# A sliding-window attention and token-MLP block on one core: single matmuls between the scores, six value blocks placed from PSUM, a new instruction order

## The chip, the cores and the metric

The kernel runs on one core of a Trainium2 chip. The time is device time in microseconds, the median of three executions. A profile is taken of one further execution; its trace gives for every engine what ran when. The engines are TensorE (PE, with its weight loads shown apart as PEld), VectorE (DVE), ScalarE (ACT), GpSimd (POOL) and SyncE (SP, which issues the transfers). Each takes its instructions in the order in which they were written for it, and waits where an input isn't there yet.

## The reference

The input x has 2048 tokens of 512 features. A vector c gives six modulation vectors. The block is a windowed attention with 32 heads of 16 features, followed by an MLP that mixes tokens (2048 tokens to 1792 hidden units and back, for each feature):

```python
mod = (_silu(c) @ w_mod).reshape(c.shape[0], 6, 1, -1)      # sa, ca, ga, sb, cb, gb
h = _layernorm(x) * (1 + ca) + sa
qkv = (h @ wqkv) ...                                        # q, k, v of 32 heads of 16
scores = einsum('bhqd,bhkd->bhqk', q, k) * Dh ** (-0.5)
mask = (i - j >= 0) & (i - j < 256)
x = x + ga * (softmax(where(mask, scores, -1e9)) @ v) @ wo
h = _layernorm(x) * (1 + cb) + sb
u = gelu(einsum('bsd,sf->bdf', _layernorm(h), w1) + b1)
x = x + gb * (einsum('bdf,fs->bds', u, w2) + b2).transpose
```

Inputs, weights and result are bf16.

## The kernel before

The tokens are worked on in four groups of 512 (`G` from 0 to 3), the heads in four sets of eight (`g8`). For each token group `proj` normalizes x (`xn`), transposes it by DMA into `h1T`, scales and shifts `h1T`, and makes Q, K and V with TensorE. A 512-wide product over the 512 features is four matmuls that add up in one PSUM bank (`pq`, `pk`, `pv`).

K and V have to be laid out with zeros between heads, so that a matmul over 32 rows meets one head only. K is cast out of PSUM into `kb` (by ScalarE or VectorE), and two instructions with the mask `mask_par` write it into `KT`. V is cast into `vb`, and two instructions with `mask_half` (the function `place`) write it into `VT`. GpSimd, which has most of these, reads the copies `kb` and `vb`.

The attention is cut into 75 chunks, counted from 0 in this text. For a chunk TensorE writes four banks of scores: three banks `pss` (one buffer) and one bank `psb` (two buffers). ScalarE exponentiates them with two instructions, `et<-pss` and `et<-psb`; the next chunk's scores can go into `pss` once the first of the two is done. VectorE multiplies the result with the window mask (`et<-et,maskt`). A unit (256 queries for one set of heads) takes the pieces of two or three chunks. Once their masks are done, TensorE multiplies with `VT` and with a matrix of ones (`po`), which gives the values and the softmax sums; ScalarE makes the reciprocal as exp(-ln) (`lz`, two instructions), and VectorE multiplies (`OT`).

`post` multiplies with the output weights (`pa`), adds the residual, normalizes (statistics `st`, then `mv`, `sq`, `rs`, `nm`; then `h`), multiplies and shifts by the modulation (`h<-h,bc_cb`, `h<-h,bc_sb`, in the text a pair of products), normalizes again and writes `hb`. From `hb` and the first MLP weights (`w1s`, `w1r`) come the hidden units `pu`: part of the sums over tokens is made early and kept in `part`, the rest follows after the attention. The tail then has Gelu (`g`), the product `guT`, and the second MLP matmul `py`, 238 matmuls with the residual added at the end.

What sets the order around all this: every step is an `Op`, made with the engines that may run it and a planned cost for each, in the order of the program. `run_schedule` emits the ops in the order of the table `ORDER`, on the engine that the table `CHOSEN` names (else the first one allowed). `Ordered` keeps each engine's instructions in that order, so all have the helper's line, L259, in the profile. Three PSUM banks (`bank`, "od") are handed round among all products that aren't scores; a new product waits for the cast that empties its bank.

TensorE's work is of three kinds: scores use it as four row tiles, values and V as four column tiles, dense products as a whole. A run of dense matmuls next to column-tiled ones is itself cut into four column tiles (`mm` with `Op.quad`), if it isn't longer than `NEAR_RUN` ops between two of them. Before, an op of a dense product holds two matmuls:

```python
for dc in (2 * n, 2 * n + 1):
    mm(
        box["q", g8][:], wqkv[:, dc, g8 * P : (g8 + 1) * P], h1T[:, dc, :],
        (dc == 0), (dc == ND - 1),
    )
...
a, z = dense("q", [0.431] * 2, e_q, h_ops, pos, alloc="od", ready=10.0)
```

## Time and profile before

| | before |
|---|---|
| median of three | 254.7 us (254.2 to 254.94) |
| profiled execution | 254.84 us |
| its span, first to last instruction | 253.1 us |
| granted TensorE clock | 0.999 |
| busy: PE, DVE, ACT, POOL | 234.0, 204.3, 179.2, 132.4 us |
| DMA | 26.86 MB, mean 106 GB/s |

The page first gives the busy time of each engine, then the span in 40 slices:

```profile
PE   7987788999988889999899899999999999999995
DVE  5597999987999989969998989899969774444443
ACT  4598999999999999999999999998138510000000
POOL 8279959999999996497159049982000000000000
```

Each digit is the busy share of 6.3 us in tenths. The first two slices are the start; ScalarE's row of nines up to about 170 us is the attention; behind it TensorE's nines stand alone.

A row of the view by line or shape reads: line, engine, operation, output and inputs by the program's names, shapes, count, busy time, mean of one in ns, then the engine's idle time just before such instructions and what ended most of it. A timeline row has the start, the length, the engine and the instruction; in brackets the idle time before it and what ended it ("issue" is a wait that the profile can't name). Rows with "x n" are n instructions in a row. A busy matmul isn't TensorE at its peak, since matmuls are pipelined.

### The profile page before, as it was taken

How to read it: one execution, taken by the hardware profiler on the slowest of the kernel's cores; microseconds unless marked ns; L12 is line 12 of the kernel's file. 1: busy time of each engine (PE TensorE's matmuls, PEld its weight loads, DVE VectorE, ACT ScalarE, POOL GpSimd, SP SyncE). 2: the span in 40 equal slices, each digit the busy share in tenths (PEclk: the TensorE clock that was granted, in tenths of full speed). 3: DMA queues.
4: the chain of work that ended last, by engine and by line, in shares of the span. 5: the costliest groups of instructions: out<-in, count | busy, mean ns of one | idle time of the engine just before them, and what ended most of it. 6: DMA issues, size and time to landing. Idle time of an engine off the chain costs nothing.

```text
span 253.1 us, 9991 instructions
## 1 busy us (share of the span) xinstructions
PE 234.0 (92%) x4385; PEld 131.6 (52%) x4385; DVE 204.3 (81%) x398; ACT 179.2 (71%) x253; POOL 132.4 (52%) x231
## 2 busy tenths in 40 slices
PE   7987788999988889999899899999999999999995
PEld 2765556655665454555555455556444444444443
DVE  5597999987999989969998989899969774444443
ACT  4598999999999999999999999998138510000000
POOL 8279959999999996497159049982000000000000
PEclk9999999999999999999999999999999999999999
DMA  6999254540173000031114821122999301111111
GB/s 204 324 351 289 52 81 26 85 109 3 23 143 93 3 5 3 3 88 44 57 33 111 225 72 52 56 84 83 295 395 386 130 23 41 41 53 50 47 41 41
DMA packets 40227, 26.86 MB, mean 106 GB/s; under 512 B 12024, under 2 KB 36088, under 8 KB 40184
## 3 DMA queue, kind: packets, MB, share of 16 engines
q1 hardware_dynamic: 40176, 26.23, 36.8%
q8 instruction: 34, 0.56, 1.0%
q14 instruction: 9, 0.07, 0.1%
q10 hardware_dynamic: 8, 0.00, 0.0%
HBM read 22.03 MB, written 2.10 MB: 95 GB/s over the span
## 4 chain that ended last, share of the span: by engine, by line
PE 39%; ACT 23%; POOL 22%; issue 7%; DVE 3%; DMA 2%; SPq 2%; POOLq 0%
ACT et L259 20%; PE py L259 19%; PE pu L259 11%; POOL h L259 7%; POOL KT L259 3%; PE pss L259 3%; POOL VT L259 3%; ACT lz L259 3%; DMA x<-in_A_x_dram 2%; POOL h1T L259 2%; POOL sq L259 2%; PE po L259 2%; POOL rs L259 2%; SPq L259 2%; PE pa L259 1%
## 5 line engine op out<-in xcount | busy, mean ns | idle before, releaser
L259 ACT ACTIVATE et<-pss 128x1536 bf16<-128x1536 f32 x75 | 111.0, 1480 | 3.9 <-PE psb L259 3.1
L259 PE MATMUL py<-guT,w2r 128*128 128x512 bf16 (+2 forms) x238 | 48.5, 366 | 0.0
L259 DVE TENSOR_TENSOR et<-et,maskt 128x1024 bf16<-128x1024 bf16 (+2 forms) x79 | 47.8, 623 | 0.4 <-ACT et L259 0.2
L259 ACT ACTIVATE et<-psb 128x512 bf16<-128x512 f32 x75 | 47.2, 630 | 0.0
L259 PE MATMUL pu<-hb,w1s 128*32 128x512 bf16 (+1 forms) x308 | 39.0, 380 | 0.7 <-POOL hb L259 0.5
L259 PE MATMUL pss<-QT,KT 32*128 32x64 bf16 (+3 forms) x720 | 30.3, 230 | 8.9 <-ACT et L259 6.0
L259 PEld LDWEIGHTS <-w2r 128*128 128x128 bf16 x238 | 22.8, 98 | 25.9
L259 PE MATMUL po<-et,VT 128*32 128x64 bf16 (+3 forms) x960 | 32.2, 233 | 1.6 <-DVE kb L259 1.1
L259 PEld LDWEIGHTS <-KT 32*128 32x128 bf16 x960 | 17.2, 92 | 30.5 <-issue 27.8
L259 PE MATMUL po<-et,ones_bd 128*32 128x256 bf16 (+3 forms) x624 | 31.4, 268 | 0.0
L259 DVE TENSOR_TENSOR otile<-py,xr 128x512 bf16<-128x512 f32 (+2 forms) x17 | 11.2, 660 | 24.4 <-PE py L259 24.3
L259 PE MATMUL psb<-QT,KT 32*128 32x64 bf16 (+3 forms) x240 | 29.4, 231 | 0.0
L259 POOL TENSOR_SCALAR VT<-vb,mask_half 128x512 bf16<-128x512 bf16 x30 | 23.3, 786 | 7.9 <-DVE vb L259 6.7
L259 PEld LDWEIGHTS <-VT 128*32 128x32 bf16 x960 | 21.8, 97 | 10.3 <-issue 3.6
L259 POOL TENSOR_SCALAR KT<-kb,mask_par 128x512 bf16<-128x512 bf16 (+1 forms) x32 | 22.4, 713 | 5.2 <-DVE kb L259 5.1
L259 PEld LDWEIGHTS <-w1s 128*32 128x32 bf16 (+1 forms) x308 | 14.2, 96 | 16.4 <-issue 2.5
L259 DVE BATCH_NORM_STATS2 st<-x 128x6 f32<-128x512 bf16 x32 | 21.4, 682 | 1.7 <-DMA x<-in_A_x_dram 1.6
L259 PE MATMUL pk<-h1T,wqkv 128*32 128x512 bf16 (+4 forms) x240 | 20.5, 342 | 2.4 <-issue 1.1
L259 PEld LDWEIGHTS <-wqkv 128*32 128x32 bf16 (+1 forms) x434 | 15.3, 96 | 11.8 <-issue 5.6
L259 PE MATMUL pv<-wqkv,h1T 128*32 128x256 bf16 x512 | 18.1, 274 | 0.2
L259 PE MATMUL pu<-hb,w1r 128*32 128x512 bf16 (+1 forms) x120 | 18.2, 379 | 0.0
L259 PE MATMUL pa<-wod,OT 128*32 128x512 bf16 (+1 forms) x148 | 16.6, 381 | 0.4 <-DVE part L259 0.2
(105 smaller groups left out, 351.5 us busy)
## 6 DMA issues: line engine op xcount, KB each, us to landing
w2r<-in_B_w_dram SPq DMA_DIRECT2D x14, 512.0 KB, 10.8
w1s<-in_B_w_dram SPq DMA_DIRECT2D x19, 256.0 KB, 3.6
w1r<-in_B_w_dram SPq DMA_DIRECT2D x9, 256.0 KB, 4.6
x<-in_A_x_dram SPq DMA_DIRECT2D x16, 128.0 KB, 4.9
wmod<-in_w_mod_dram SPq DMA_DIRECT2D x4, 512.0 KB, 7.2
out_dram<-otile SPq DMA_DIRECT2D x15, 128.0 KB, 1.7
wmod<-in_w_mod_dram SPq DMA_DIRECT2D x4, 256.0 KB, 3.6
wqkv<-in_A_wqkv_dram SPq DMA_DIRECT2D x4, 256.0 KB, 5.4
```

The lines of the kernel that those rows point to most:

```text
L259: ins = call(*args, **kwargs)
```

## The change

An op of a dense product now holds one matmul in place of two (`q`, `k`, `pa`, `pu`, the early `part` sums); for V, two of the four feature blocks of a half. The value products and the sums of a unit are two ops, `e_av` and `e_sum`, where they were one. `NEAR_RUN` goes from 7 to 14. Six of the V blocks (`DIRECT_V`: two for each of the token groups 1 to 3) are placed into `VT` straight from PSUM by two instructions, without `vb`, and give up their bank after the second. The planner is told that ScalarE may place K and V (`masked`) and normalize. `DIRECT_K`, the same for K, is empty. `ORDER` and `CHOSEN` are new. The arithmetic is the same.

```diff
-NEAR_RUN = 7
+NEAR_RUN = 14
+DIRECT_V = [(1, 2), (1, 3), (2, 2), (2, 3), (3, 2), (3, 3)]
+DIRECT_K = []
 ORDER = [
-    46, 44, 47, 45, 48, 49, 51, 50, 52, 65, 53, 119, 66, 54, 120, 75, 67, 70, 55, 68, 71, 121, 76, 69, 56, 72, 123,
+    46, 44, 47, 45, 48, 49, 51, 50, 52, 65, 53, 127, 66, 54, 128, 75, 67, 76, 55, 68, 70, 129, 71, 69, 56, 131, 72,
...
+        elif e == "ACT":
+            ac.activation(out=dst, in_=src, func=ACT.Identity, scale=rs[:, i : i + 1], bias=nm[:, i : i + 1])
...
-    def values(dst, h1T, tb, n):
+    def values(dst, h1T, tb, n, dcs):
-        for dc in range(ND):
+        for dc in dcs:
...
+    def masked(e, out, in_, mask):
+        if e == "ACT":
+            ac.activation(out=out, in_=in_, func=ACT.Copy, scale=mask)
+        else:
+            ENGINE[e].tensor_scalar(out=out, in0=in_, scalar1=mask, scalar2=0.0, op0=ALU.mult, op1=ALU.add)
...
-                for dc in (2 * n, 2 * n + 1):
-                    mm(
-                        box["q", g8][:], wqkv[:, dc, g8 * P : (g8 + 1) * P], h1T[:, dc, :],
-                        (dc == 0), (dc == ND - 1),
-                    )
+                mm(box["q", g8][:], wqkv[:, n, g8 * P : (g8 + 1) * P], h1T[:, n, :], (n == 0), (n == ND - 1))
-            a, z = dense("q", [0.431] * 2, e_q, h_ops, pos, alloc="od", ready=10.0)
+            a, z = dense("q", [0.2155] * 4, e_q, h_ops, pos, alloc="od", ready=10.0)
...
+            if (G, tb) in DIRECT_V:
+                placed = [
+                    op("vd", {"ACT": 0.5, "DVE": 0.61}, 0.5,
+                       lambda e, half=half: place(e, VT[r3], box["v", tb], tb, half), deps=[z] + war, pos=pos)
+                    for half in range(2)
+                ]
+                a.frees = placed
...
-        engine, shifted = ({"POOL": 0.77, "DVE": 0.35}, True) if G < POOL_POST else ({"DVE": 0.34}, False)
+        engine, shifted = ({"POOL": 0.77, "DVE": 0.35, "ACT": 0.5}, True) if G < POOL_POST else ({"DVE": 0.34}, False)
...
+        for cost, emit, needs in ((0.005 + 0.0001 * len(mine), e_av, vs), (0.007 + 0.0001 * len(runs), e_sum, [])):
+            av = op("AV", "PE", columns + cost, emit, deps=ready + needs + av_chain[-1:],
+                    pos=i + AV_POS, cls="AV", alloc=None if unit["avs"] else "od")
...
-            for sc in range(lo, NT, 2):
+            for sc in range(lo, NT):
```

How the new tables move instructions is seen on the engines that wait for each other. In all, VectorE has 12 placings `VT<-pv` where it had none, 6 V casts fewer, 3 Q casts fewer (they go to ScalarE) and 4 pairs of products fewer; GpSimd has 12 V placings and 6 K placings fewer and those 4 pairs more; TensorE has 66 matmuls more, since more of the dense products are cut into column tiles.

ScalarE, in the first chunks. `et<-pss` and `et<-psb` are the exponentials of a chunk; before:

```order
L259 ACTIVATE et<-pss 128x1536
L259 ACTIVATE et<-psb 128x512
L259 ACTIVATE rs<-mv,eps_t 128x2
L259 ACTIVATE rs<-rs 128x2
L259 ACTIVATE kb<-pk 128x256
L259 ACTIVATE et<-pss 128x1536
L259 ACTIVATE et<-psb 128x512
L259 ACTIVATE et<-pss 128x1536
L259 ACTIVATE et<-psb 128x512
L259 ACTIVATE vb<-pv 128x512
L259 ACTIVATE et<-pss 128x1536
```

and with the change:

```order
L279 ACTIVATE et<-psb 128x512
L279 ACTIVATE QT_1_148<-pk 128x256
L279 ACTIVATE rs<-mv,eps_t 128x2
L279 ACTIVATE rs<-rs 128x2
L279 ACTIVATE QT_2_149<-pk 128x256
L279 ACTIVATE et<-pss 128x1536
L279 ACTIVATE kb<-pk 128x256
L279 ACTIVATE et<-psb 128x512
L279 ACTIVATE et<-pss 128x1536
L279 ACTIVATE QT_3_150<-pk 128x256
L279 ACTIVATE vb<-pv 128x512
L279 ACTIVATE et<-psb 128x512
```

Three Q casts are new among the first three chunks. On TensorE, in the same place, 8 of the 16 K/Q matmuls between the scores of chunks 3 and 4 move behind those of chunk 4.

VectorE, around the masks of chunks 23 to 26 (the V of token group 2 is `VT_169`), before:

```order
L259 CAST vb<-pv 128x512
L259 TENSOR_TENSOR et<-et,maskt 128x4x256
L259 CAST kb<-pk 128x512
L259 TENSOR_TENSOR et<-et,maskt 128x4x128
L259 CAST vb<-pv 128x512
L259 TENSOR_SCALAR h_2314<-x_68,rs,nm 128x512
L259 TENSOR_SCALAR h_2337<-x_67,rs,nm 128x512
L259 TENSOR_TENSOR et<-et,maskt 128x4x256
L259 CAST vb<-pv 128x512
L259 TENSOR_TENSOR h_2314<-h_2314,bc_cb_118 128x512
L259 TENSOR_TENSOR h_2314<-h_2314,bc_sb 128x512
```

and with the change:

```order
L279 CAST kb<-pk 128x512
L279 TENSOR_TENSOR et<-et,maskt 128x4x256
L279 TENSOR_SCALAR VT_169<-pv,mask_half 128x32x16
L279 TENSOR_TENSOR OT_0_140<-po,lz 128x256
L279 TENSOR_SCALAR VT_169<-pv,mask_half 128x32x16
L279 TENSOR_SCALAR h_2401<-x_68,rs,nm 128x512
L279 CAST QT_1_148<-pq 128x512
L279 TENSOR_TENSOR et<-et,maskt 128x4x128
L279 TENSOR_TENSOR et<-et,maskt 128x4x256
L279 TENSOR_SCALAR VT_169<-pv,mask_half 128x32x16 x2
```

Two V casts became four placings from PSUM, and the pair of products went to GpSimd.

GpSimd, in the same stretch, before:

```order
L259 TENSOR_SCALAR KT_3_162<-kb,mask_par 128x16x32 x2
L259 TENSOR_SCALAR h_2351<-x_66,rs,nm 128x512
L259 TENSOR_SCALAR VT_169<-vb,mask_half 128x32x16 x2
L259 TENSOR_SCALAR h_2439<-x_65,rs,nm 128x512
L259 TENSOR_TENSOR h_2337<-h_2337,bc_cb_118 128x512
L259 TENSOR_TENSOR h_2337<-h_2337,bc_sb 128x512
L259 TENSOR_SCALAR KT_1_164<-kb,mask_par 128x16x32 x2
L259 TENSOR_TENSOR h_2351<-h_2351,bc_cb_118 128x512
L259 TENSOR_TENSOR h_2351<-h_2351,bc_sb 128x512
L259 TENSOR_SCALAR VT_169<-vb,mask_half 128x32x16 x2
L259 TENSOR_SCALAR KT_0_163<-kb,mask_par 128x16x32 x2
L259 TENSOR_SCALAR VT_169<-vb,mask_half 128x32x16
```

and with the change:

```order
L279 TENSOR_SCALAR KT_3_162<-kb,mask_par 128x16x32 x2
L279 TENSOR_TENSOR h_2314<-h_2314,bc_cb_118 128x512
L279 TENSOR_TENSOR h_2314<-h_2314,bc_sb 128x512
L279 TENSOR_SCALAR xn<-x_80,rs,nm 128x512
L279 TENSOR_SCALAR h_2581<-x_66,rs,nm 128x512
L279 TENSOR_TENSOR h_2581<-h_2581,bc_cb_118 128x512
L279 TENSOR_TENSOR h_2581<-h_2581,bc_sb 128x512
L279 TENSOR_TENSOR h_2736<-h_2736,bc_cb_118 128x512
L279 TENSOR_TENSOR h_2736<-h_2736,bc_sb 128x512
L279 TENSOR_SCALAR KT_0_163<-kb,mask_par 128x16x32 x2
L279 TENSOR_SCALAR VT_169<-vb,mask_half 128x32x16
```

The V and K placings thin out, and three pairs of products stand in a row where two stood apart.

More of the change, by code (lines that the diff above doesn't have):

```diff
@@ L877, in v @@
             ve_op = b
-            b = op("vp", {"POOL": 1.5, "DVE": 0.68}, 1.45, e_vp, deps=[b], pos=pos)
+            b = op("vp", {"POOL": 1.5, "DVE": 0.68, "ACT": 1.0}, 1.45, e_vp, deps=[b], pos=pos)
             slot(vb_tag, ve_op, b)
@@ L998, in k @@
-            a.frees = [b]
-            mms.append(z)
-            if not direct:
-                ke = b
-                b = op("kk", {"POOL": 1.38, "DVE": 0.68}, 1.75, lambda e: split(ENGINE[e], box["kb", g8]), deps=[ke] + war, pos=pos)
-                slot(kb_tag, ke, b)
-            k_done[2 * G, g8] = k_done[2 * G + 1, g8] = [b]
+                done = [
+                    op("kd", {"ACT": 0.5, "DVE": 0.61}, 0.5, lambda e, par=par: split(e, box["k", g8], par), deps=[z] + war, pos=pos)
+                    for par in range(2)
+                ]
@@ new lines, in value @@
+        def value(xy, kb, q, width, col):
+            block = 4 * unit["H"] + kb
+            new = "ps" not in unit
+            if new:
+                unit["ps"] = bank([P, 2, HQ], F32, "po")
+            for j in range(4):
+                te.matmul(
+                    unit["ps"][32 * j : 32 * j + 32, xy, q : q + width],
+                    lhsT=ones_bd[:] if xy else VT[block // 8 % 3][:, block % 8, 4 * unit["g8"] + j, :],
+                    rhs=et_of[c][:, j, col : col + width], start=new, stop=True,
+                    tile_position=(0, 32 * j), skip_group_check=True,
+                )
```

165 lines of the change are left out of this document (64 added, 101 removed), and 132 rows, old and new, of tables (CHOSEN, ORDER).

## The prediction

> **What bounds the kernel now.** I read the page's busy times first, then the busy time by stage, then ScalarE's timeline inside the attention stage, the waits, and last the chain that ended last.
>
> ```profile
> PE 234.0 (92%) x4385; PEld 131.6 (52%) x4385; DVE 204.3 (81%) x398; ACT 179.2 (71%) x253; POOL 132.4 (52%) x231
> ...
> core 0: us, PE busy (x) PEld busy (x) DVE busy (x) ACT busy (x) POOL busy (x), PEclk, DMA share, GB/s
> ...
> 41.00:103.00 62.00, 56.52 (x1566) 34.69 (x1558) 57.46 (x106) 60.87 (x83) 55.95 (x76) 1.00 0.25 48
> 103.00:170.00 67.00, 63.53 (x1560) 36.10 (x1560) 61.41 (x111) 66.31 (x89) 43.94 (x64) 1.00 0.28 78
> 170.00:201.00 31.00, 31.00 (x329) 15.64 (x322) 27.22 (x62) 17.33 (x32) 2.62 (x4) 1.00 0.76 263
> ```
>
> TensorE's 92% is a mean over two regimes. From 170 on TensorE is busy without a gap (31.00 of 31.00, and in the rows of the chain below on to the last output) and alone sets the end. Before that, ScalarE is full: 60.87 of 62 and 66.31 of 67 us. So the kernel is 75 chunks paced by ScalarE, and a tail of pure matmuls. The tail is fixed work, so time can be won only if the 75 chunks pass faster, or if work from the tail goes into them. What one chunk costs stands in ScalarE's timeline:
>
> ```profile
> 160.66 1.45 ACT L259 ACTIVATE et<-pss 128x1536 bf16<-128x1536 f32 x1
> 162.01 0.38 ACT L259 ACTIVATE lz<-po 128x256 f32<-128x256 f32 x1
> ...
> 162.75 0.43 ACT L259 ACTIVATE lz<-lz 128x256 f32<-128x256 f32 x1
> 163.06 1.46 ACT L259 ACTIVATE et<-pss 128x1536 bf16<-128x1536 f32 x1
> ...
> 165.03 1.45 ACT L259 ACTIVATE et<-pss 128x1536 bf16<-128x1536 f32 x1
> ...
> 166.85 0.39 ACT L259 ACTIVATE lz<-po 128x256 f32<-128x256 f32 x1
> 167.12 1.47 ACT L259 ACTIVATE et<-pss 128x1536 bf16<-128x1536 f32 x1
> ...
> 162.41 0.28 PE L259 MATMUL pss<-QT,KT 32*128 32x256 bf16 x3
> ...
> 164.58 0.26 PE L259 MATMUL pss<-QT,KT 32*128 32x192 bf16 x3
> ```
>
> From one `et<-pss` to the next it is 1.97 us with no `lz` between (163.06 to 165.03), 2.09 with one, 2.40 with two. TensorE needs 2.17 (162.41 to 164.58) where 1.71 us of other matmul columns stand between two scores, so heavy chunks are TensorE's and light ones ScalarE's. Whatever is longer than this table is a stall. The stalls stand in the waits:
>
> ```profile
> 20.51 0.83 PE L259 MATMUL pk<-h1T,wqkv 128*128 128x256 bf16 x6 [1.09 <-issue]
> 21.72 1.45 ACT L259 ACTIVATE et<-pss 128x1536 bf16<-128x1536 f32 x1 [1.14 <-PE psb L259]
> ...
> PE po L259 <- DVE kb L259: 1.1, 2, 0.6
> PE pu L259 <- POOL hb L259: 0.5, 1, 0.5
> PE pk L259 <- DVE vb L259: 0.5, 1, 0.5
> PE pq L259 <- DVE kb L259: 0.4, 1, 0.4
> ...
> by line: POOL h L259 22.1%; POOL KT L259 18.1%; POOL VT L259 10.4%; POOL h1T L259 7.9%; POOL rs L259 7.2%; ACT et L259 6.9%; POOL hb L259 6.5%; issue 6.5%; PE pu L259 4.9%; POOL mv L259 4.2%; POOL sq L259 3.9%; PE pss L259 1.6%; POOL nm L25
> ```
>
> The first two rows are between the scores of chunks 3 and 4, where TensorE stands 1.09 us amid its K/Q matmuls and ScalarE 1.14. The four waits fall between 78 and 96 us and sum to 2.5 us; the last row is the chain of waits in that stretch, and it runs almost wholly through GpSimd. These 3.6 us are what the change can reach.
>
> **The change part by part.** I work against the profiled execution, 254.84 us (span 253.1 and 1.74 around it); the median, 254.7, is 0.14 lower.
>
> *Matmul work and tail: -0.2.* Counting matmul columns in the two instruction orders, at 0.2158 us for a 512-column matmul (22.88 us over 106 in the row below), the columns up to the last scores, without the scores' own, differ by one matmul, 110.3 us against 110.1; the work behind the last scores falls by the same 0.2. Single matmuls instead of pairs thus even out the chunks (of three with 1.92 us of columns two fall to 1.49 or less; the last before the tail rises to 2.13) but move nothing more out of the tail.
>
> ```profile
> 178.94 22.88 PE pu L259 x106
> 201.82 48.40 PE py L259 x238
> ```
>
> In all, pricing the 61 chunks 13 to 73 by the table above, by their `lz` and their load, gives 127.8 us for the old order and 127.7 for the new. The finer cut alone is worth 0.1, from which I take 0. More column-tiled quartets (66 more matmuls) cost no columns. The Trainium skill, "TensorEngine Tiling (Array Packing)", Key Properties, says that a change of tiling mode drains TensorE; the new order has 155 such changes where there were 153. By the 2.17 less 1.71 us above, which holds the scores and two changes, two more cost at most 0.46 us, and by that rule the sum would be 253.7. The heavy and the light chunks of the table hold their changes already, so the sum goes without it.
>
> *The stall behind chunk 3: -0.4.* Half of the K/Q matmuls there (8 of 16) move behind the scores of chunk 4, so the 1.09 us no longer stands ahead of them: at most 1.14 us for ScalarE, at least 0 if the wait comes back one chunk on. Against it ScalarE takes three Q casts of 256 columns from VectorE. Such a cast takes ScalarE
>
> ```profile
> 13.96 0.37 ACT L259 ACTIVATE kb<-pk 128x256 bf16<-128x256 f32 x1
> ```
>
> 0.37; one falls into a wait for statistics, two lie on the loop: +0.7. ScalarE places and normalizes nothing: the instruction order shows none there, so that part of the change is only a permission.
>
> *GpSimd's relief: -2.5.* Prices by shape:
>
> ```profile
> L259 POOL TENSOR_SCALAR VT<-vb,mask_half 128x512 bf16<-128x512 bf16 x30 | 23.3, 786 | 7.9 <-DVE vb L259 6.7 <-ACT vb L259 1.2
> L259 POOL TENSOR_SCALAR KT<-kb,mask_par 128x512 bf16<-128x512 bf16 x18 | 14.8, 832 | 0.0
> L259 POOL TENSOR_TENSOR h<-h,bc_sb 128x512 bf16<-128x512 bf16 x7 | 8.6, 1222 | 0.5
> L259 POOL TENSOR_TENSOR h<-h,bc_cb 128x512 bf16<-128x512 bf16 x7 | 8.2, 1169 | 0.3
> ...
> 91.21 1.66 POOL h1T L259 x2
> ```
>
> Up to the first `hb` GpSimd loses 7 V placings (5.5 us), 4 whole and 4 half K placings (3.3 and, at half a whole one, 1.7) and gains one more pair of products on `h` (2.4) and two `h1T` (1.66 by the last row): 6.4 us less. That is far more than the 0.5 us that TensorE waited for `hb`, and the waits for `kb` and `vb` came out of the same crowd. All of the 2.5 can go; nothing of it goes if VectorE is as late as before.
>
> *VectorE's load: +1.5.* This is where the work goes. A V block that was one cast on VectorE and two placings on GpSimd is two placings from PSUM on VectorE. No such operation is in the trace; the nearest rows are
>
> ```profile
> L259 DVE CAST vb<-pv 128x512 bf16<-128x512 f32 x15 | 10.2, 679 | 0.9 <-PE pv L259 0.9
> L259 DVE TENSOR_SCALAR bcs<-ps_b,bc_fix 128x512 bf16<-128x512 f32 x1 | 0.8, 799 | 0.0
> L259 DVE TENSOR_SCALAR VT<-vb,mask_half 128x512 bf16<-128x512 bf16 x2 | 0.7, 342 | 0.0
> L259 DVE TENSOR_TENSOR h<-h,bc_cb 128x512 bf16<-128x512 bf16 x9 | 4.0, 447 | 0.0
> L259 DVE TENSOR_TENSOR h<-h,bc_sb 128x512 bf16<-128x512 bf16 x9 | 6.3, 704 | 0.3
> ```
>
> Reading PSUM it cannot be under 0.679 (the cast of the same tile) and should not be over 0.799; I take 0.70, so a block costs 1.40 where it cost 0.68. Between the masks of chunks 13 and 42 (41 to 103 us) the new order has on VectorE 6 placings from PSUM (+4.2), 2 fewer from SBUF (-0.7), 4 fewer V casts (-2.7), one pair of products fewer (-1.2) and some ten more changes (2 statistics fewer; more `part`, Q, `wod`, K placings and normalizing, most at the cast's 0.68; +4.6 together): +4.2 us of durations. Instructions in a row overlap (the mask of 0.68 below starts 0.60 ahead of the next one), which makes it some +3.7. VectorE is busy 57.46 of 62 there, so 4.5 us are free, but much of that is waiting in order for inputs. Bounds: 0, if all fits in, and 3.7. I take 1.5, below the middle, because masks stand ahead of their products, as in the mask that ends at 75.1 for value matmuls that start at 80.17:
>
> ```profile
> 74.43 0.68 DVE L259 TENSOR_TENSOR et<-et,maskt 128x1024 bf16<-128x1024 bf16 x1
> 75.03 0.41 DVE L259 TENSOR_TENSOR OT<-po,lz 128x256 bf16<-128x256 f32 x1
> ...
> 80.17 0.41 PE L259 MATMUL po<-et,VT 128*32 128x256 bf16 x8
> ```
>
> From 103 on VectorE has some 2 us less work than before, and 5.6 us were free: 0. The sum: 254.84 - 0.2 - 0.4 - 2.5 + 1.5 = 253.24, and by the median's 0.14 some 253.1; I forecast 253.2.
>
> **The rivals.** *VectorE sets the pace.* GpSimd's product pairs hold VectorE up:
>
> ```profile
> 76.95 1.16 POOL L259 TENSOR_TENSOR h<-h,bc_sb 128x512 bf16<-128x512 bf16 x1
> 77.00 1.66 DVE L259 TENSOR_TENSOR et<-et,maskt 128x1024 bf16<-128x1024 bf16 x1
> 79.31 1.05 PE L259 MATMUL pk<-h1T,wqkv 128*32 128x512 bf16 x16 [0.54 <-DVE vb L259]
> ```
>
> A mask of 0.68 takes 1.66 beside such a product; the V cast behind it comes late, and TensorE stands 0.54. The new order has 22 such products on GpSimd, not 14, and more of VectorE's work around them. The place is the stage from 41 to 103: 57.46 busy plus 3.7 is 61.2 of 62, and whatever of the free 4.5 stays as waiting comes on top. The price is then in the upper half of its bounds, 2.8 at the middle of it, and none of the 2.5 is won: 254.84 + 2.8 - 0.4 - 0.2 = 257.0. It decides once VectorE is later than the lead of its masks over the value matmuls. Against it: 18 placings on GpSimd go. The Trainium skill, "SBUF — State Buffer", section Who interferes with whom, states the same as a rule: a VectorE instruction with two SBUF inputs and a GpSimd one that reads SBUF share a port and one blocks the other wholly; the rows at 77 agree, and since it leaves out an instruction with at most one SBUF input outside the two-port modes, it also says that the new placings are free of it.
>
> *The stalls only move.* ScalarE's loop is the same length (127.7), and a later wait for VectorE takes the place of each old one: only -0.4 and -0.2 are left, 254.2, within what can't be told from no change. For it: in the old kernel the waits name VectorE more often than GpSimd.
>
> *All stalls go.* VectorE's additions fit into its free time: 254.84 - 0.2 - 0.4 - 2.5, and the rest of the 1.14 at the start if the casts hide (0.7): 251.0. Against it: it needs VectorE at 61.2 of 62.
>
> *The change does not do what it says*: true only for ScalarE's part, and already in the sum.
>
> **How the numbers follow.** Chances: forecast 0.38, VectorE's pace 0.25, stalls move 0.23, all stalls go 0.14. The range that leaves about 2 in 10 out reaches from just under the best case, 250.9, to a little over the price of VectorE's pace, 257.2; the forecast's own range is 252.2 to 254.2. What a measurement here can tell from no change is about 0.3%, 0.76 us: faster is below 253.94, slower above 255.46. Faster: 0.32 of the forecast's 0.38, all of the best case, 0.03 of the case that stalls move: 0.49. Same: 0.06 and 0.17 of these: 0.23. Slower: 0.25 and 0.03: 0.28.
>
> **What would show it.** Right: no 1.1 us gap of ScalarE before its fifth `et<-pss`; no wait for POOL `hb`; VectorE busy 60 us or more of the 62 in the middle stage; the last scores about 1.5 us earlier, and the tail from there to the end as long as now. Wrong: `po`, `pv` or `pk` waiting for VectorE by more than 2.5 us between 40 and 105; placings from PSUM over 0.8 us; or a gap of TensorE behind 170, which the sum has at nothing because its only cover is that `hb` of the last tokens is done before TensorE runs out of other products.

## The result, and the profile after

| | median us (runs) | ratio to before, 95% interval |
|---|---|---|
| before | 254.82 (4) | |
| with the change | 260.74 (260.71 to 261.29, 4) | 1.0241 (1.0218 to 1.0264) |

The change makes the kernel 2.4% slower, where 0.6% faster was forecast; the range ended at 257.2. The profiled span grew from 253.1 to 258.9 us. In all tables the medians are over all runs; the ratios leave out two of the ten runs of the kernel called g4 below, which took 259.04 and 259.41 us at a mean clock of 0.987 where the other eight took 253.53 to 254.51. The page of the changed kernel gives the engines' busy times, the granted clock over the 40 slices, and the shares of the chain that ended last:

```profile
PE 235.8 (91%) x4451; PEld 132.1 (51%) x4451; DVE 211.8 (82%) x403; ACT 180.4 (70%) x256; POOL 120.6 (47%) x217
...
PEclk9999999999999999997999999999999999999999
...
PE 51%; DVE 20%; ACT 11%; issue 7%; DMA 5%; POOL 4%; SPq 1%; DVEq 0%; POOLq 0%; ACTq 0%
```

GpSimd is 11.8 us less busy, as the change wanted, and its share of the chain, 22% before, is down to 4%. But VectorE is 7.5 us busier, though it has only five instructions more, and it now holds a fifth of the chain. And one digit of the clock row is a 7.

Cut at the starts of chunks 13, 47, 49 and of the last scores, the two kernels compare like this (per engine: busy us and number of instructions; then the clock). First before, then the changed kernel:

```profile
10.86:40.83 29.97, 24.45 (x629) 17.30 (x628) 28.00 (x63) 27.86 (x39) 22.70 (x43) 1.00 0.75 189
40.83:113.39 72.56, 66.53 (x1822) 40.66 (x1821) 65.79 (x119) 71.42 (x96) 64.52 (x90) 1.00 0.24 49
113.39:117.60 4.21, 3.85 (x104) 2.27 (x101) 4.14 (x9) 4.21 (x7) 2.70 (x4) 1.00 0.21 62
117.60:171.38 53.78, 51.22 (x1253) 29.02 (x1254) 50.42 (x93) 53.10 (x72) 34.22 (x50) 1.00 0.30 82
171.38:253.10 81.72, 78.82 (x514) 37.57 (x510) 50.41 (x98) 17.61 (x32) 1.24 (x2) 1.00 0.36 126
```

```profile
10.87:40.92 30.05, 25.14 (x720) 17.52 (x719) 27.98 (x65) 28.90 (x42) 21.64 (x40) 1.00 0.79 196
40.92:114.09 73.17, 65.67 (x1790) 40.19 (x1787) 69.64 (x122) 71.22 (x96) 53.42 (x79) 1.00 0.22 50
114.09:123.01 8.92, 5.46 (x114) 3.08 (x111) 8.45 (x14) 4.75 (x7) 5.32 (x5) 0.81 0.12 32
123.01:177.36 54.35, 51.77 (x1245) 28.87 (x1242) 49.64 (x86) 52.80 (x71) 33.20 (x49) 1.00 0.29 80
177.36:258.90 81.54, 78.66 (x529) 37.77 (x525) 50.51 (x100) 17.69 (x32) 0.16 (x1) 1.00 0.36 123
```

The tail is 0.2 us shorter, as forecast. The last scores start 6.0 us later, where 1.5 us earlier was forecast. Of that, 4.7 us come from chunks 47 and 48 alone, which take 8.92 us instead of 4.21 (of the rest, 0.6 in chunks 13 to 46 and 0.6 behind chunk 48); TensorE is busy for 5.46 of these and ScalarE for 4.75, VectorE for 8.45. In chunks 13 to 46 VectorE is 3.9 us busier (69.64 for 65.79) with three instructions more.

What happened in chunks 47 and 48 is read from the timelines of the changed kernel. VectorE first, with a K placing pair at another place (79.65) for comparison, then GpSimd, TensorE and ScalarE; the bracket is the engine's idle time before the row, and what ended it:

```profile
79.65 0.61 DVE L279 TENSOR_SCALAR KT<-kb,mask_par 128x512 bf16<-128x512 bf16 x2
...
111.16 2.13 DVE L279 TENSOR_TENSOR et<-et,maskt 128x512 bf16<-128x512 bf16 x2
...
114.14 1.24 DVE L279 TENSOR_SCALAR h<-x,rs,nm 128x512 bf16<-128x512 bf16 x1
115.31 2.46 DVE L279 TENSOR_SCALAR KT<-kb,mask_par 128x512 bf16<-128x512 bf16 x2
117.69 0.68 DVE L279 COPY part<-pu 128x512 f32<-128x512 f32 x1
...
114.02 1.22 POOL L279 TENSOR_TENSOR h<-h,bc_cb 128x512 bf16<-128x512 bf16 x1
115.32 1.15 POOL L279 TENSOR_TENSOR h<-h,bc_sb 128x512 bf16<-128x512 bf16 x1
116.42 1.20 POOL L279 TENSOR_TENSOR h<-h,bc_cb 128x512 bf16<-128x512 bf16 x1
117.70 1.15 POOL L279 TENSOR_TENSOR h<-h,bc_sb 128x512 bf16<-128x512 bf16 x1
...
113.34 0.82 PE L279 MATMUL pu<-hb,w1s 128*32 128x512 bf16 x12
118.43 0.29 PE L279 MATMUL po<-et,VT 128*32 128x128 bf16 x8 [2.96 <-DVE part L279]
120.89 1.52 PE L279 MATMUL pu<-hb,w1s 128*32 128x512 bf16 x12
...
119.20 1.45 ACT L279 ACTIVATE et<-pss 128x1536 bf16<-128x1536 f32 x1 [2.30 <-PE psb L279]
```

Read from the top: the pair of K placings that takes 0.61 us takes 2.46 at 115.31, and each of its two instructions ends 0.15 us behind a product on GpSimd (the products end at 116.47 and 117.62, the placings at 116.62 and 117.77). The scaling of h ahead of it ends at 115.38, 0.15 behind the product of 114.02 (115.24). `part`, which reads PSUM and not SBUF, takes its usual 0.68 beside a product over its whole length. TensorE's value matmuls of chunk 47 need one of the three PSUM banks that all products share, and get the one that `part` empties; so they stand 2.96 us, the next scores stand behind them in TensorE's order, and ScalarE runs dry for 2.30. Behind the wait the same 12 `pu` matmuls take 1.52 us instead of 0.82: that is the 7 in the clock row.

So it was a chain: products on GpSimd, a VectorE queue held up by them, a late copy that frees a bank, TensorE, ScalarE, and then the clock. It had to be told apart from the simpler reading that VectorE has too much work, for which the placings from PSUM would be to blame.

### The profile page after: what moved, and what is told of

Same layout as the page of the kernel before. It is cut to its first block, busy times and chain, and to the rows that moved or that the text cites. A ratio compares the mean times of both kernels' runs of the same rounds, so it can differ in the third digit from the quotient of the medians.

```text
span 258.9 us, 10127 instructions
## 1 busy us (share of the span) xinstructions
PE 235.8 (91%) x4451; PEld 132.1 (51%) x4451; DVE 211.8 (82%) x403; ACT 180.4 (70%) x256; POOL 120.6 (47%) x217
## 4 chain that ended last, share of the span: by engine, by line
PE 51%; DVE 20%; ACT 11%; issue 7%; DMA 5%; POOL 4%; SPq 1%; DVEq 0%; POOLq 0%; ACTq 0%
PE py L279 19%; PE pu L279 15%; ACT et L279 9%; DVE et L279 6%; PE po L279 5%; PE pss L279 4%; PE pa L279 4%; PE pv L279 3%; DVE st L279 2%; DMA x<-in_A_x_dram 2%; ACT lz L279 2%; DVE kb L279 2%; DVE VT L279 2%; DVE h L279 2%; POOL hb L279 1%
## 5 line engine op out<-in xcount | busy, mean ns | idle before, releaser
L279 DVE TENSOR_TENSOR et<-et,maskt 128x1024 bf16<-128x1024 bf16 (+2 forms) x79 | 52.2, 684 | 0.8 <-ACT et L279 0.5
L279 PE MATMUL pu<-hb,w1s 128*32 128x512 bf16 (+1 forms) x302 | 42.5, 393 | 1.7 <-DVE part L279 1.2
L279 PE MATMUL po<-et,ones_bd 128*32 128x256 bf16 (+3 forms) x624 | 32.3, 271 | 0.0
L279 PEld LDWEIGHTS <-KT 32*128 32x128 bf16 x960 | 16.6, 92 | 29.1 <-issue 25.4
L279 POOL TENSOR_SCALAR KT<-kb,mask_par 128x512 bf16<-128x512 bf16 (+1 forms) x26 | 18.1, 707 | 13.5 <-DVE kb L279 11.2
L279 PE MATMUL pk<-h1T,wqkv 128*32 128x512 bf16 (+4 forms) x297 | 21.8, 332 | 1.2 <-DVE OT L279 0.4
L279 PE MATMUL pu<-hb,w1r 128*128 128x512 bf16 (+1 forms) x111 | 19.3, 380 | 0.0
L279 PEld LDWEIGHTS <-ones_bd 128*32 128x32 bf16 x624 | 16.0, 98 | 3.1 <-issue 0.4
```

The lines of the kernel that those rows point to most:

```text
L279: ins = call(*args, **kwargs)
```

## The experiments

The medians, each beside the runs of the kernel before on the same chip; "more" is the distance of the two medians (5.9 us for the changed kernel), "span" is that of the profiled execution. The rows come from different chips, and the kernel before has medians from 253.97 to 254.82 us there, so rows are compared by their distance or ratio and not by their medians:

| kernel | median us (runs) | before beside it | more | ratio, 95% interval | span |
|---|---|---|---|---|---|
| e1 two pairs on VectorE | 257.78 (4) | 254.19 | +3.6 | 1.0157 (1.0128 to 1.0185) | 255.2 |
| e2 one-input products | 254.29 (1) | 254.19 | +0.1 | one run | 252.6 |
| e3 before, two pairs on GpSimd | 255.59 (10) | 254.19 | +1.4 | 1.0052 (1.0027 to 1.0077) | 252.8 |
| e4 three instructions moved | 259.19 (4) | 254.19 | +5.0 | 1.0203 (1.0167 to 1.0240) | 258.0 |
| f1 fillers in the wait | 259.17 (4) | 253.97 | +5.2 | 1.0240 (1.0186 to 1.0293) | 257.1 |
| f2 all pairs on VectorE | 258.05 (4) | 253.97 | +4.1 | 1.0163 (1.0130 to 1.0197) | 256.7 |
| f3 V placed by GpSimd again | 264.48 (4) | 253.97 | +10.5 | 1.0411 (1.0377 to 1.0446) | 262.1 |
| f4 six pairs and order | 258.30 (6) | 253.97 | +4.3 | 1.0170 (1.0135 to 1.0205) | 256.9 |
| g2 three pairs and order | 260.17 (6) | 254.33 | +5.8 | 1.0230 (1.0186 to 1.0274) | 256.7 |
| g5 order only | 258.65 (4) | 254.33 | +4.3 | 1.0177 (1.0129 to 1.0225) | 256.8 |
| g3 before, one-input products | 253.32 (10) | 254.33 | -1.0 | 0.9963 (0.9931 to 0.9995) | 249.5 |
| g4 as e2, timed | 254.13 (10) | 254.33 | -0.2 | 0.9989 (0.9961 to 1.0018) | 252.6 |
| h1 four one-input for a pair | 256.28 (4) | 254.20 | +2.1 | 1.0079 (1.0048 to 1.0110) | 254.0 |

**e1, two product pairs back on VectorE.**

```diff
 "DVE":  [ ..., 557, 563, ...
+          558, 562,
 "POOL": [ ..., 
-          558, 562,
```

> The changed kernel with two of its eleven product pairs on h (those that GpSimd works off from 114 to 119 us) back on VectorE; nothing else moved. Theory A (contention): GpSimd's two-input products hold VectorE's SBUF instructions until each product ends, which makes the two K placings at 115.3 take 2.46 us where 0.61 is usual, makes `part` behind them late, and TensorE's 2.96 us wait for `part` and the half clock behind it come from that. Then the K placings fall to 0.6 to 0.9 us, the wait to under 0.8, the clock stays at 1.00, and the time falls by 3.5 to 5 us, to 255.7 to 257.2, although VectorE gets 1.7 us more work there. Theory B (VectorE simply has too much work there, by the change's placings from PSUM): 1.7 us more work makes the wait longer, and the time rises by 1 to 2 us, to 262 or more.

VectorE's and TensorE's timelines of e1 at the same place:

```profile
114.18 0.60 DVE L280 TENSOR_SCALAR KT<-kb,mask_par 128x512 bf16<-128x512 bf16 x2
...
115.43 0.30 PE L280 MATMUL po<-et,VT 128*32 128x128 bf16 x8 [0.63 <-DVE part L280]
117.14 0.40 PE L280 MATMUL pu<-hb,w1s 128*32 128x512 bf16 x4 [0.98 <-DVE QT L280]
120.92 0.81 PE L280 MATMUL pu<-hb,w1s 128*128 128x512 bf16 x3 [0.55 <-DVE part L280]
```

The placings are back at 0.60, the 2.96 are 0.63, the clock of the profiled execution stays whole, and the kernel is 3.6 us slower than before instead of 5.9, with 1.7 us *more* work on VectorE. That is against the reading by amount of work. The median, 257.78, is 0.6 above the range that I expected: a part of the lateness comes back in the next two waits.

**e2 and g4, the products with one input.** The scale and shift of the second normalization are left out for the eleven tiles on GpSimd; count and order of instructions stay.

```diff
 def e_m(e, tl=tl):
     u = h2[tl]
+    if e == "POOL":
+        po.tensor_scalar(out=u[:], in0=u[:], scalar1=1.0, scalar2=0.0, op0=ALU.mult, op1=ALU.add)
+        po.tensor_scalar(out=u[:], in0=u[:], scalar1=1.0, scalar2=0.0, op0=ALU.mult, op1=ALU.add)
+        return
```

> The changed kernel with GpSimd's eleven product pairs (two SBUF inputs each) made one-input instructions with a constant, so that the scale and shift of the second normalization are left out for these eleven tiles. GpSimd's queue keeps the same count and order. Theory A (the second input is what holds VectorE up): masks and placings beside them lengthen by some tenths only, as beside GpSimd's other one-input work (in the changed kernel 3.8 us over 116 instructions, against 12.5 over 43 beside the products); the 2.96 us wait is under 0.8 and the time is 253 to 256.5. Theory C (any GpSimd work on SBUF holds VectorE up as much): the K placings at about 115 stay over 1.5 us, the wait stays over 2 us, and the time is within 1.5 us of 260.7.

> The changed kernel with one-input products once more, timed against the kernel before on the chip that runs its counterpart: 253.5 to 255.5 by its one run of 254.29. Against the kernel before with the same edit it should be within 1.5 us either way.

The 2.96 us wait is gone (0.4 are left in e2), and so is the whole loss: 254.13 in the median, beside 254.33 for the kernel before. VectorE's and GpSimd's rows of e2:

```profile
112.83 1.40 DVE L279 TENSOR_SCALAR KT<-kb,mask_par 128x512 bf16<-128x512 bf16 x2
...
112.00 2.79 POOL L279 TENSOR_SCALAR h<-h 128x512 bf16<-128x512 bf16 x4
```

The placings still take 1.40, not 0.61: one-input instructions hold them too, but each is 0.67 us long where a product is 1.2. Each of the two placings again ends 0.14 to 0.15 us behind the GpSimd instruction beside it. e2 does not say whether the second input counts, or the length, or how long GpSimd works on the pairs in all; h1 below takes up the last of these.

**g3, the same edit in the kernel before** (scale and shift left out for its seven tiles on GpSimd).

> The kernel before with its seven GpSimd product pairs made one-input instructions (their scale and shift left out), the same edit as in the changed kernel: what the rest of the change is worth once the products hold nobody up. Before has few stalls beside its products (4.9 us of lengthening over 28 instructions, hidden for the most part), so I expect 252.5 to 254.3. If it stays near 254, the rest of the change (finer matmul work, V from PSUM) gains nothing over it; if it comes out over 255, the changed order gains more than a microsecond wherever the products are harmless.

253.32: the kernel before gains 1.0 us by it, the changed one 6.1 (from 5.9 us above the kernel before to 0.2 below). With the products made harmless the two differ by 0.8 us (253.32 and 254.13, beside the same runs of before), and the intervals of their ratios overlap. So no gain by the rest of the change shows here, and no loss either.

**e3, one part of the change alone**, in the kernel before: ops 476 and 478 from VectorE to GpSimd.

```diff
 "POOL": [ ..., 
+          476, 478,
```

> The kernel before with only one part of the change: the two product pairs that VectorE did between 119 and 125 us go to GpSimd. Theory A (contention): VectorE has 1.7 us less work there, and yet its masks and copies beside the products lengthen by 2 us or more in all, and the kernel is no faster, most likely 1 to 4 us slower: 255.5 to 259. Theory B (VectorE's load is what counts): the kernel gains from the relief or stays: 253.5 to 254.8.

0.5% slower, with 1.7 us less work on VectorE, and just inside the first range. The profiled execution is one of the fastest of e3's ten (254.50 us). Of the timelines of e3, VectorE's, GpSimd's and TensorE's:

```profile
121.21 1.98 DVE L260 TENSOR_TENSOR et<-et,maskt 128x1024 bf16<-128x1024 bf16 x2
...
121.32 1.59 POOL L260 TENSOR_TENSOR h<-h,bc_sb 128x512 bf16<-128x512 bf16 x1
...
126.86 1.05 PE L260 MATMUL pk<-h1T,wqkv 128*32 128x512 bf16 x16 [1.09 <-DVE vb L260]
```

Two masks take 1.98, of which one is 0.70 longer than alone, and GpSimd's own product stretches to 1.59. What TensorE pays, 1.09, comes by another way than in chunk 47: the statistics that stand ahead of the V cast in VectorE's queue wait 1.04 us, with VectorE idle, for the last product, which GpSimd ends at 125.50. So products on GpSimd cost the kernel before something too, here more by coming late than by holding VectorE up; the 2 us of lengthening that I expected are not in this trace.

**f3, the V placings back on GpSimd** in the changed kernel: a cast on VectorE and two placings from SBUF on GpSimd, for all six blocks (with one buffer for the cast).

```diff
+def e_vd(half):
+    if ("vx", tb) not in box:
+        box["vx", tb] = work.tile([P, 2, 256], BF, name="vb", tag="vx", bufs=1)
+        copy("DVE", box["vx", tb][:], box["v", tb][:])
+    place("POOL", VT[r3], box["vx", tb], tb, half)
...
-    lambda e, half=half: place(e, VT[r3], box["v", tb], tb, half)
+    lambda e, half=half: e_vd(half)
```

> The changed kernel with the six value blocks as they were before: one cast on VectorE and two placings from SBUF on GpSimd, in the same order of everything. VectorE loses 4.8 us of work (12 placings of 0.74 for 6 casts of 0.68), GpSimd gains 12 placings of about 0.78. Theory A (the products on GpSimd make the loss): the stall of chunk 18 (0.85 us) may go, those beside the products stay or come at other places, and the time is 258.5 to 262. Theory B (the placings from PSUM load VectorE too much): the time falls by 3 us or more, to 257.7 or less.

10.5 us slower than the kernel before where the changed kernel is 5.9: the other side of what "too much work on VectorE" asks for, and beyond both ranges that I gave. The stage from 41 to 103 us in the changed kernel, and then in f3:

```profile
41.00:103.00 62.00, 54.90 (x1535) 34.29 (x1539) 59.38 (x105) 60.10 (x82) 45.55 (x66) 1.00 0.22 50
```

```profile
41.00:103.00 62.00, 53.20 (x1448) 32.86 (x1443) 53.57 (x97) 57.30 (x77) 53.35 (x72) 0.97 0.24 50
```

VectorE is 5.8 us less busy there (53.57 for 59.38), and the chunks still pass more slowly: ScalarE, which sets their pace, gets 57.30 us of work done instead of 60.10. The single buffer adds to that by an amount the run does not separate, and so does a stretch of 3.4 us at half clock in this stage, which the changed kernel does not have there (a clock of 0.97 for 1.00 in the two rows). So f3 does not show what the placings from PSUM cost in all. What the traces do show is that nothing holds them up. The changed kernel has all twelve at nearly the same length, 0.73 to 0.75 us, and in g5 one that runs wholly beside a product takes 0.74:

```profile
L279 DVE TENSOR_SCALAR VT<-pv,mask_half 128x512 bf16<-128x512 f32 x12 | 8.7, 739 | 0.0
```

**f1, TensorE kept busy in its wait.** Ten matmuls on constants go ahead of the waiting value matmuls, into the bank that chunk 48's scores take next.

```diff
-                box["sa"] = ps_a.tile([P, 3, D], F32, name="pss")
+                if i != 48:
+                    box["sa"] = ps_a.tile([P, 3, D], F32, name="pss")
...
+def filled(e, emit=ops[727].emit):
+    box["sa"] = ps_a.tile([P, 3, D], F32, name="pss")
+    for n in range(10):
+        te.matmul(box["sa"][:, 0, :], lhsT=identity[:], rhs=nothing[:], start=True, stop=True, skip_group_check=True)
+    emit(e)
+ops[727].emit = filled
```

> The changed kernel with ten more matmuls of 512 columns (on constants, into the score bank, overwritten by the next scores) issued just ahead of the value matmuls that wait 2.96 us for `part`, so that TensorE is busy for about 2.2 of these microseconds; the wait for `part` itself is untouched. Theory D (the half clock behind the wait comes from TensorE's standing still, and costs about 2 us of the 4.67 that chunks 47 and 48 lose): the value matmuls start as late as before, the clock stays at or near 1.00 from 118 to 124 us, chunk 48 takes 2.2 to 2.8 us instead of 4.25, and the time falls by 1.4 to 2.1 us, to 258.6 to 259.4. Rival (the clock costs nothing, since TensorE waits for VectorE there anyway): the time stays within 0.5 us of 260.7.

TensorE's timeline of f1:

```profile
115.86 2.32 PE L279 MATMUL pss<-nothing,identity 128*128 128x512 bf16 x9 [0.70 <-ACT et L279]
118.12 0.29 PE L279 MATMUL po<-et,VT 128*32 128x128 bf16 x8
...
120.00 0.83 PE L279 MATMUL pu<-hb,w1s 128*32 128x512 bf16 x12
```

The value matmuls start as late as ever, 4.34 us into the chunk as in the changed kernel (118.43 less 114.09), but the 12 `pu` matmuls behind them are back at 0.83, and chunk 48 takes 2.76 us for 4.25. So the trace shows the half clock, and its 1.5 us, gone. The total shows it less surely. The median is 1.6 us below that of the changed kernel, but beside the kernel before f1 is 5.2 us slower for 5.9, and its ratio, 1.0240, is that of the changed kernel, 1.0241: one of the four runs, at 261.75, had a mean clock of 0.993 again, and the other three, at 1.000, lie between 258.83 and 259.45.

**e4, g5, g2, f4, f2: can it be mended by order, or by moving more pairs?** e4 and g5 leave all pairs on GpSimd and move instructions that free banks ahead; g2 moves three pairs, f4 six, f2 all eleven.

```diff
 e4  - 557 ... 1175, 874, ..., 1176, 563, ..., 904, ..., 566
     + 1175, 1176, 557, ..., 904, ..., 566, 563, 874
 g5  + 233 ahead of 387; 463 behind 618; 1176 behind 1175; 557, 874, 566, 558 behind 898; 563 behind 885; 839 behind 1254
 g2  + "DVE": 281, 558, 562; 233, 463, 839 as in g5; 281 behind 658; 557, 874 behind 1176; 562, 566 behind 898; 563, 558 behind 885
 f4  + "DVE": 277, 281, 558, 562, 842, 844; 1176, 557, 874 behind 1175; 562, 563 behind 718; 277 behind 618; 844 behind 1002
 f2  + "DVE": 277, 279, 281, 558, 560, 562, 564, 838, 840, 842, 844
```

> The changed kernel with three VectorE instructions in another order and all products left on GpSimd: the copy `part` goes ahead of the scaling of h, and the two K placings and one more scaling of h go behind the Q cast, the masks and the OT product. Theory A with its queue part (TensorE waits for a PSUM bank that `part` frees, and `part` stands behind the held-up placings in VectorE's queue): the 2.96 us wait falls to under 1, the clock does not drop or drops less, and the time falls by 2.5 to 5 us, to 255.7 to 258.2, with the products still beside the placings. Theory B (too much work on VectorE): the order changes little; the wait moves to the masks or the Q cast, and the time is within 1 us of 260.7.

> The changed kernel with all eleven pairs left on GpSimd and only the order on VectorE changed: the same moves in chunks 18, 28 and 67, and in chunk 47 `part` and the Q cast ahead of both scalings of h and the K placings. If the queue order is the larger half of the loss, 254.5 to 257; if the products on GpSimd hold up whatever stands there, the masks of chunks 47 to 49 are late instead and it is 257.5 to 260.

> The changed kernel with three product pairs (chunks 31 and 47) on VectorE, set behind the masks, casts and copies that free PSUM banks, and at four places an instruction that frees a bank moved ahead of one that does not: the OT product of chunk 18 ahead of a mask, the V placings of chunk 28 ahead of a mask, `part`, the K placings and the Q cast of chunk 47 ahead of products and scalings, and a scaling of h behind `part` in chunk 67. Theory (what stands ahead of a bank-freeing instruction in VectorE's queue, and how long GpSimd holds it, makes the stalls): chunk 18 falls from 2.96 to 2.1, 28 from 2.92 to 2.1, 33 from 2.73 to 2.2, 47 to 50 from 13.0 to 8.7 or less, 67 from 3.2 to 2.6, and the time is 252.5 to 255. Rival (VectorE is full, and each stall only moves to another chunk, as in the kernel with six pairs moved): 257 or more.

> The changed kernel with the six product pairs whose neighbours stall TensorE (chunks 28, 31, 47, 48, 67) on VectorE, the other five on GpSimd, and the copy `part`, the K placings and the Q cast of chunk 47 ahead of the scaling and the products of h. If both parts of theory A hold (products beside VectorE's SBUF work hold it up, and what stands behind it in VectorE's queue holds PSUM banks), the stalls of these chunks go (0.85, 0.3, 4.67, 1.06 us and some of chunk 33) and the time is 252.5 to 255, so no slower than the kernel before. If VectorE's amount of work decides, it is 257 or more.

> The changed kernel with all eleven of GpSimd's product pairs on VectorE at the same places in the order. Theory A (contention): VectorE takes 9.1 us of work (11 pairs at 0.83) and loses up to 12.5 us of being held up; the stalls of chunks 28, 31, 33, 47, 48 and 67 go or shrink, against new lateness where VectorE is full: 254 to 257. Theory B (VectorE's amount of work decides): 9.1 us more make it 262 or more.

(The numbers are those of the order table. 233 is the OT product of chunk 18, 387 and 463 are masks, 618 is a V placing of chunk 28, 1175 the `pu` matmul ahead of `part`, 1176 `part`, 557, 563 and 839 are scalings of h, 874 the K placings of 115.31, 904 a Q cast, 566 a statistic, 718 an OT product, 885 a V placing, 898 a K cast, 658 a Q cast, 1002 a mask, 1254 a `part`; the others are product pairs.)

All five end between 258.05 and 260.17, and none came into the better of its expectations. f4 and g2 fell into the range that I had given for "VectorE's amount of work decides" and "VectorE is full", g5 into the one for "the masks are late instead"; e4 and f2 lie between their two. Lengths from score to score (of the profiled executions, from the starts of the first score matmuls):

| chunks | before | changed | e4 | g5 | g2 | f4 | f2 | e2 |
|---|---|---|---|---|---|---|---|---|
| 18 to 30 | 27.24 | 28.76 | 28.79 | 28.35 | 28.35 | 30.82 | 28.72 | 27.96 |
| 31 to 37 | 16.82 | 15.58 | 15.56 | 15.72 | 16.52 | 14.91 | 15.85 | 14.91 |
| 47 to 51 | 10.44 | 15.02 | 13.74 | 13.11 | 13.25 | 11.90 | 11.01 | 11.09 |
| 67 to 73 | 15.35 | 16.51 | 16.49 | 16.82 | 16.82 | 16.59 | 16.06 | 15.27 |

Three of these hold a stretch of 3.4 us at half clock: 47 to 51 of the changed kernel and of e4, 18 to 30 of f4.

Where I moved the bank-freeing instruction ahead, its own stall went (chunk 18 from 2.96 to 2.13, 47 from 4.67 to 2.08, 67 from 3.23 to 2.17 us in g5 and g2), and the next one came late instead. In g5, VectorE and TensorE behind chunk 67:

```profile
163.41 3.54 DVE L280 TENSOR_TENSOR et<-et,maskt 128x512 bf16<-128x512 bf16 x3
...
167.93 0.40 PE L280 MATMUL po<-et,VT 128*32 128x256 bf16 x8 [1.38 <-DVE OT L280]
```

Three masks, the first two of them beside GpSimd's last two products, take 3.54 us in all; the OT product behind them frees its bank 1.38 us late. VectorE is nearly full for several chunks on either side (in g5 busy for 93% of chunks 60 to 66 and 98% of 67 to 73), so what is lost comes up at whichever bank is asked for next. Moving all pairs (f2) takes the products' hold-ups away but puts 10.6 us of products on VectorE: chunks 47 to 51 are nearly mended, and chunks 38 to 46, which had been fine (18.59), take 19.89. No version that computes everything beat the kernel before. So the products on GpSimd make the stall of chunk 47 (e1), and without products of that length nothing is lost (g4); but bringing pairs back to VectorE does not bring the time back, since VectorE is then full. How much of that fullness is the new placings and how much the new order, no run here separates; f3, which was made for the placings, ran with a single buffer.

**h1, length or amount.** Each pair becomes four one-input instructions on GpSimd (scale and shift left out).

```diff
-        po.tensor_scalar(out=u[:], in0=u[:], scalar1=1.0, scalar2=0.0, op0=ALU.mult, op1=ALU.add)
-        po.tensor_scalar(out=u[:], in0=u[:], scalar1=1.0, scalar2=0.0, op0=ALU.mult, op1=ALU.add)
+        for _ in range(4):
+            po.tensor_scalar(out=u[:], in0=u[:], scalar1=1.0, scalar2=0.0, op0=ALU.mult, op1=ALU.add)
```

> The changed kernel with each of GpSimd's eleven product pairs replaced by four one-input instructions of the same shape in a row (scale and shift left out), so that GpSimd is busy at least as long per pair (4 times 0.67 us is 2.7, the pair took 2.4) but each instruction is short and has one input. Theory F (a held-up VectorE instruction waits until the GpSimd instruction that runs beside it ends, so the length of one instruction counts, and whether it has one or two inputs): the K placings beside them take 1.2 to 1.6 us instead of 2.46 and the time is 254 to 256.5. Theory G (what counts is how long GpSimd works on SBUF in all): the stall of chunk 47 comes back, and the time is 258.5 or more.

GpSimd's groups in the changed kernel (its products) and in h1, and the K placings of h1 beside them:

```profile
L279 POOL TENSOR_TENSOR h<-h,bc_cb 128x512 bf16<-128x512 bf16 x11 | 13.7, 1246 | 4.4 <-DVE h L279 4.1
L279 POOL TENSOR_TENSOR h<-h,bc_sb 128x512 bf16<-128x512 bf16 x11 | 13.2, 1202 | 0.9
```

```profile
L279 POOL TENSOR_SCALAR h<-h 128x512 bf16<-128x512 bf16 x44 | 31.3, 716 | 5.1 <-DVE h L279 2.1
...
112.97 1.48 DVE L279 TENSOR_SCALAR KT<-kb,mask_par 128x512 bf16<-128x512 bf16 x2
```

GpSimd works longer on these pairs than in the changed kernel (31.3 us for 26.9), and the kernel is 2.1 us slower than before: 3.8 us better than with products, 2.3 worse than with half as many one-input instructions. So GpSimd's time in all counts, and the length or kind of one instruction counts besides: more time in all, and yet faster. The two placings take 0.78 us each here and 1.31 and 1.23 beside the products, and all four end 0.14 to 0.15 us behind the GpSimd instruction beside them: what is held up waits for that one instruction, some 0.6 us long here, 1.2 there. Whether a two-input instruction of 0.7 us would hold VectorE as little was not tried.

## Why the prediction was wrong, step by step

**The step that failed is "From 103 on VectorE has some 2 us less work than before, and 5.6 us were free: 0".** It counted VectorE's work by the durations that its instructions have alone. Chunks 47 to 73 lie in that stage; the step puts them at 0, and they took 5.3 us more, 4.7 of it in chunks 47 and 48. The free time was real (61.41 busy of 67 before), but three product pairs fall on the 8.6 us from 110.3 to 118.9, and what they hold up is not in any count of instructions. To size it, take for every VectorE instruction beside a product its duration less the shortest of its form: 5.2 us over 26 instructions before, 12.5 over 40 in the changed kernel, with 1.9 of it in the K placings of 115.31. By this count eleven pairs on GpSimd cost VectorE about 1.1 us each, while a pair that it does itself costs it 0.83 (0.41 and 0.42 in e1; 0.93 in f2, where it does all sixteen). Work moved off an engine cost that engine as much as doing it, or more.

**The rival "VectorE sets the pace" had the mechanism, in the wrong place and at less than half the price.** It named the products that hold masks up, and the 22 instead of 14 of them, but it put the place at 41 to 103, where VectorE was fullest, and the price at 2.8 us, taken from VectorE's added durations there. Chunks 13 to 46 lost 0.6 us in all. It also spoke of masks only, which read two SBUF inputs; in chunk 47 a scaling of h and two K placings, with one, were held as well. The price was made where the products stand in a row and a bank-freeing copy stands behind them.

**"The price is then in the upper half of its bounds" and the term of +1.5 for VectorE's load** rested above all on the placings from PSUM. They measured 0.739 us (I took 0.70), and no more beside GpSimd's work. Chunks 18 to 30 did take 1.5 us more (28.76 for 27.24), but that this is the size of the term is chance: in e2, with harmless products and the same placings, 0.7 are left. The stall that no product makes is chunk 18, 0.9 us: it is the same in e1, e2 and f2 (3.02, 2.97 and 2.97 for 2.07 before), and it goes when the OT product moves ahead of a mask (2.13 in g5).

**GpSimd's relief, -2.5.** The four waits did shrink: chunks 31 to 37 take 15.58 us for 16.82. That is half of the term, and the reason was not the one I gave, or not it alone. In g3, where GpSimd keeps all its V and K placings and only the products become short, the same chunks take 15.33 (one profile, of the fastest of ten runs). So the waits of 78 to 96 us that I put down to GpSimd's crowd of placings can go without moving a placing. Whether the products made them by holding VectorE up or by filling GpSimd, g3 does not separate.

**The stall behind chunk 3, -0.4.** It went (3.44 us to 2.32), but it is also gone in e3 and g3 (2.32 both), whose program is the one before up to there. It was an event of the one profiled execution, not of the order; I had built a term on one row without a second execution to hold it against. Chunks 0 to 12 took 0.1 us more in all, and executions of one and the same early order spread by more than that (29.3 to 30.6 us with the change, 28.8 to 30.0 before), so the runs can't size this term.

**The tail, -0.2**, was right: 81.72 to 81.54 us. ScalarE's gap of 1.1 us and the wait for GpSimd's `hb` went, as stated; VectorE busy 60 of 62 was nearly so (59.38). The sign that should have warned was the other one stated, waits for VectorE between 40 and 105: they came to 2.2 us, under the 2.5 that I had set (3.2 with `pa` and `pq`, which I had left out), and the loss came ten microseconds later.

**The half clock** was in no step. It is 1.5 of the 4.7 us (chunk 48 with and without it, 4.25 and 2.76).

The Trainium skill, "SBUF — State Buffer", section Who interferes with whom, was weighed in the rival. Its rule that one of the two engines blocks for the whole instruction of the other agrees with the K placings that end with GpSimd's products (2.46 for 0.61). Its exemption, of instructions with at most one SBUF input outside the two-port modes, agrees with `part` (0.68) and, in g5, a V placing from PSUM (0.74) beside them; that the K placings, with one SBUF input, are held agrees with it only if they run in such a mode, which no run here shows. What was lacking was the rule's price in this order, and that it reaches further than the masks.

## What to carry to other kernels

Before you move work from VectorE to GpSimd, look at what VectorE does beside it: two-input products of 1.2 us on GpSimd lengthened VectorE's masks, scalings and placings from SBUF by up to 1.0 us each, in all about as much as the products would have cost there, while instructions that read PSUM kept their length (0.68 and 0.74 us). Moving them back helps only while VectorE still has room. Price a stage's free time with the hold-ups in it, and ask which instruction behind the held one frees a PSUM bank that TensorE's next matmul needs. And a term that rests on a single stall of a single profiled execution needs a second execution.

## What the runs showed of the hardware that was not expected

TensorE's clock fell to half without a long standstill. It fell at 119.3 us of the changed kernel and came back 3.4 us later:

```profile
119.00:119.40 0.40, 0.16 (x8) 0.09 (x1) 0.40 (x2) 0.20 (x1) 0.40 (x1) 0.92 0.00 0
119.40:119.80 0.40, 0.14 (x4) 0.13 (x7) 0.40 (x2) 0.40 (x1) 0.17 (x1) 0.50 0.00 0
...
122.20:122.60 0.40, 0.40 (x21) 0.40 (x17) 0.14 (x1) 0.00 (x0) 0.00 (x0) 0.50 0.00 0
122.60:123.00 0.40, 0.40 (x19) 0.18 (x7) 0.40 (x1) 0.00 (x0) 0.00 (x0) 0.82 0.00 0
```

The longest gap ahead of it was 2.96 us. In e4 the longest was 1.89, in f4 1.68, in f3 at 87 us 1.05, and the clock fell all the same. What these have in common is TensorE's busy time in the 3.4 us before: 0.7 us in the changed kernel, 1.5 in e4, 1.4 in f4, 1.3 and 0.5 in f3. Where no stretch of 3.4 us between the start and the tail had less than 1.6 (g2 1.63, g5 1.72, e1 1.77), the profiled execution kept its clock; in e3 it kept it with 1.56. The Trainium skill, "TensorE: Matmul & The Clock Gate", Part 1, ties the half rate to an idle window of about 3.4 us; here a window less than half busy was enough in five places, but not in e3's. So it is no sharp limit, and the clock of one kernel falls in some executions and not in others: of g2's six runs three had a clock of 0.993 and took 260.64 to 261.23 us, three 1.000 and took 258.43 to 259.70.
